# Re-timing the steps of an attention stage: later divisors, weight additions on DVE, two-bank hash bits, another order of loads

## The chip, the cores and the metric

The kernel runs on one core of one Trainium2 chip. The metric is the device time of one execution in microseconds. A figure "in the trace" is from one profiled execution.

Engines: PE does matrix products, DVE and ACT elementwise work, POOL (GpSimd) here weight additions and some transfers, and SP's queue issues most transfers (DMA). In the timelines below each queue's transfers stand in the order in which the kernel asks for them (SP: rd at 290.39, r at 293.85, q at 295.04 us). A "hole" below is a stretch in which PE waits.

## The reference

```python
def _attn_ref(q, k, v, proj):              # q, k, v: 4 x 8 heads x 768 x 64, proj: 64 x 6
    q_bits = (np.einsum('bhsd,dk->bhsk', q, proj) > 0)      # 6 hash bits of a row
    k_bits = (np.einsum('bhsd,dk->bhsk', k, proj) > 0)
    mask = bucket(q_bits)[:, :, :, None] == bucket(k_bits)[:, :, None, :]
    scores = np.where(mask, scale * np.matmul(q, k.transpose(0, 1, 3, 2)), -1e9)
    attn = np.exp(scores - np.max(scores, axis=-1, keepdims=True))
    attn = attn / (np.sum(attn, axis=-1, keepdims=True) + 1e-09)
    return np.matmul(attn, v)

def _moe_ref(x, w_in, w_out):              # x: 3072 x 512, w_in: 512 x 2048, w_out: 2048 x 512
    h = x @ w_in
    sp = np.maximum(h, 0.0) + np.log1p(np.exp(-np.abs(h)))
    return (h * erf(sp)) @ w_out
```

(Shortened; `bucket` stands for the sum of bits times powers of two.) The attention output, transposed, is the x of the feed-forward.

## The kernel before

Attention works on 16 pairs of heads. A pair takes four steps, n = 4i + r with r = 0 to 3: two halves of the queries, each with two groups of keys. A step's PE work is the scores of step n, part of the hash bits of pair i + 1, and the weighing of the values by the exponentials of step n - 1. After each half, the key sums become the divisors z. Once a pair, z is spread over partitions by a trip through DRAM (`zd`, `zc`), inverted on DVE, sent through DRAM again (`rd`, `r`) and multiplied in. Beside that, the feed-forward weights are loaded in 32 pieces of 512 KB and rounded by ACT, DVE and POOL, one piece in two steps.

```python
def hash_bits(d, r, bitp):                 # one half of q or k a step, in one PSUM bank
    what, half = ("q", "q", "k", "k")[r], r % 2
    # ...
    ps = bank("bits", 1)[:, 0:HS]
    nc.tensor.matmul(out=ps, lhsT=proj_sb, rhs=d[what][:, cols], start=True, stop=True)
    return what, cols, ps

def invert(i):
    # ...
    nc.vector.tensor_scalar(out=zc, in0=zc, scalar1=S * EPS, scalar2=None, op0=ALU.add)
    nc.vector.reciprocal(out=zc, in_=zc)
    rd = dram.tile([2, S], F32, name="rd", tag="rd")
    nc.sync.dma_start(out=rd[:, :].rearrange(...), in_=zc)              # arguments cut
    d["r"] = norm.tile([P, S], F32, name="r", tag="r")
    for ab in range(2):
        nc.sync.dma_start(out=d["r"][...], in_=rd[ab : ab + 1, :].broadcast_to([D, S]))

for n in range(NS + 4):
    i, r = divmod(n, 4)
    if n < NS:
        if r == 0 and i >= 1 and i + 1 < NPAIR:
            pairs[i + 1] = fetch(i + 1, load)      # q, k, v on the sync queue, three buffers
        scores(n)
        taking = bits(i + 1, r) if i + 1 < NPAIR else None
    if 1 <= n <= NS:
        sum_keys(n - 1)
        weigh(n - 1)
    if n < NS:
        exponentials(n)
        if taking:
            taking()
    if 1 <= n <= NS and (n - 1) % 2 == 1:
        divisor(n - 1)                             # PE needs the sums that DVE has just begun
        leave(n - 1)
    if r == 0 and i >= 1:
        spread(i - 1)
    if r == 2 and i >= 1:
        invert(i - 1)
    if r == 3 and i >= 1:
        normalise(i - 1)
    if n % 2 == 0:
        round_weights(n // 2, 0)
    else:
        round_weights(n // 2, 1)                   # ends with the addition, on POOL
        fetch_weights(n // 2 + 2)                  # on POOL's queue, behind that addition
```

Of the kernel before, what the change touches and what calls it, by code (L numbers as in the profile page):

```python
# [37 lines left out]
F32 = mybir.dt.float32  # L38
BF16 = mybir.dt.bfloat16
I32 = mybir.dt.int32  # L40
U32 = mybir.dt.uint32
AF = mybir.ActivationFunctionType
ALU = mybir.AluOpType
# [3 lines left out]
P = 128  # L47
# [16 lines left out]
def kernel(  # L64
# [11 lines left out]
    nc = tc.nc  # L76
    B, H, S, D = v.shape
# [17 lines left out]
    const = ctx.enter_context(tc.tile_pool(name="const", bufs=1))  # L95
    dram = ctx.enter_context(tc.tile_pool(name="dram", bufs=2, space=bass.MemoryType.DRAM))
    psum = ctx.enter_context(tc.tile_pool(name="psum", bufs=3, space=PSUM))
    proj_sb = const.tile([P, P], F32, name="proj_sb")
    kcol_sb = const.tile([P, 2], F32, name="kcol_sb")
    ones = const.tile([P, D], F32, name="ones")  # L100
# [7 lines left out]
    nc.vector.memset(proj_sb, 0.0)  # L108
    for ab in range(2):
        for c in range(2):  # L110
            nc.sync.dma_start(
                out=proj_sb[ab * D : ab * D + D, ab * D + c * NBIT : ab * D + (c + 1) * NBIT],
                in_=proj2[ab * D : ab * D + D, ab * NBIT : (ab + 1) * NBIT],
            )
# [27 lines left out]
    def big(name):  # L142
        return psum.tile([P, 2, 512], F32, name=name, tag="big", bufs=3)

    def bank(name, which):
        return psum.tile([P, 512], F32, name=name, tag=f"bank{which}", bufs=1)
# [34 lines left out]
            )  # L181
        return d

    def hash_bits(d, r, bitp):

        what, half = ("q", "q", "k", "k")[r], r % 2
        cols = slice(half * HS, (half + 1) * HS)
        if half == 0:
            d[what + "b"] = bitp.tile([P, S], BF16, name=what + "b", tag=what + "b")
        ps = bank("bits", 1)[:, 0:HS]  # L190
        nc.tensor.matmul(out=ps, lhsT=proj_sb, rhs=d[what][:, cols], start=True, stop=True)  # L191
        return what, cols, ps

    def take_bits(d, what, cols, ps):
        dst = d[what + "b"][:, cols]
        if what == "q":
            nc.scalar.activation(out=dst, in_=ps, func=AF.Sign, scale=2.0**100, bias=sgn[:, 0:1])
        else:
            nc.vector.tensor_scalar(
                out=dst,  # L200
                in0=ps,
                scalar1=kcol_sb[:, 0:1],
                scalar2=kcol_sb[:, 1:2],
                op0=ALU.is_gt,
                op1=ALU.mult,
            )

    def attention():
        NS = NPAIR * 4
        with (  # L210
# [1 line left out]
            tc.tile_pool(name="bitp", bufs=2) as bitp,  # L212
            tc.tile_pool(name="ep", bufs=1) as ep,
            tc.tile_pool(name="sums", bufs=2) as sums,
            tc.tile_pool(name="norm", bufs=1) as norm,
            tc.tile_pool(name="small", bufs=3) as small,
            tc.tile_pool(name="rawp", bufs=2) as rawp,
            tc.tile_pool(name="cvt", bufs=1) as cvt,
        ):
# [6 lines left out]
            def fetch_weights(n):  # L226
                if n >= len(pieces):
                    return
                if not WIDE:
                    nc.gpsimd.dma_start(out=pieces[n][0], in_=pieces[n][1])  # L230
                else:
                    raws[n] = rawp.tile([P, WP, 2], I32, name="raw", tag="raw")
                    nc.gpsimd.dma_start(
                        out=raws[n][:, :, :].rearrange("p c two -> p (c two)"), in_=pieces[n][1]
                    )

            def round_weights(n, part):
# [7 lines left out]
                if part == 0:  # L245
# [44 lines left out]
                    op0=ALU.mult,  # L290
                    op1=ALU.mult,
                )
                nc.gpsimd.tensor_tensor(
                    out=pieces[n][0], in0=top[:, :].bitcast(F32), in1=rest, op=ALU.add
                )
                raws.pop(n)
# [26 lines left out]

            def sum_keys(n):
                d = pairs[n // 4]
                es = [etiles[(n * GC + c) % len(etiles)][:, :, 0:HS] for c in range(GC)]
                if n % 2 == 0:
                    d["sum"] = sums.tile([P, 2, HS], F32, name="sum", tag="sum")
                    nc.vector.tensor_tensor(out=d["sum"], in0=es[0], in1=es[1], op=ALU.add)
                    es = es[2:]  # L330
                for e in es:
                    nc.vector.tensor_tensor(out=d["sum"], in0=d["sum"], in1=e, op=ALU.add)  # L332

            def weigh(n):
                half, g = n // 2 % 2, n % 2
# [14 lines left out]
                        )  # L350

            def divisor(n):
                d = pairs[n // 4]
                z = d["z_ps"] = bank("z_ps", 1)[:, 0:HS]
                for ab in range(2):
                    nc.tensor.matmul(  # L356
                        out=z[ab * D : ab * D + D, :],
                        lhsT=ones,
                        rhs=d["sum"][:, ab, :],
                        start=True,  # L360
                        stop=True,
                    )

            def leave(n):

                half = n // 2 % 2
                d = pairs[n // 4]
                b, j = divmod(n // 4, JP)
                cols = slice(half * HS, (half + 1) * HS)
                nc.scalar.copy(out=xT[b][:, j, cols], in_=d["av"][:, 0:HS])  # L370
                if half == 0:
                    d["ev"] = small.tile([P, 1], F32, name="ev", tag="ev")
                    nc.vector.tensor_scalar(
                        out=d["ev"],
                        in0=d["av"][:, HS : HS + 1],
                        scalar1=EPS,
                        scalar2=None,
                        op0=ALU.mult,
                    )
                    d["z"] = norm.tile([P, S], F32, name="z", tag="z")  # L380
                nc.scalar.copy(out=d["z"][:, cols], in_=d["z_ps"])

            def spread(i):

# [33 lines left out]
                    out=x, in0=x, scalar=d["ev"][:, 0:1], in1=d["r"], op0=ALU.add, op1=ALU.mult  # L418
                )

            def bits(i, r):
                what, cols, ps = hash_bits(pairs[i], r, bitp)
                return lambda: take_bits(pairs[i], what, cols, ps)

            for i in range(2):
                pairs[i] = fetch(i, load)
            for n in range(2):
                fetch_weights(n)
            for r in range(4):
                bits(0, r)()  # L430
            for n in range(NS + 4):
                i, r = divmod(n, 4)
                if n < NS:
                    if r == 0 and i >= 1 and i + 1 < NPAIR:
                        pairs[i + 1] = fetch(i + 1, load)
                    scores(n)
                    taking = bits(i + 1, r) if i + 1 < NPAIR else None
                if 1 <= n <= NS:
                    sum_keys(n - 1)
                    weigh(n - 1)  # L440
                if n < NS:
                    exponentials(n)
                    if taking:
                        taking()
                if 1 <= n <= NS and (n - 1) % 2 == 1:
                    divisor(n - 1)
                    leave(n - 1)
                if r == 0 and i >= 1:
                    spread(i - 1)
                if r == 2 and i >= 1:  # L450
                    invert(i - 1)
                if r == 3 and i >= 1:
                    normalise(i - 1)
                if n % 2 == 0:
                    round_weights(n // 2, 0)
                else:
                    round_weights(n // 2, 1)
                    fetch_weights(n // 2 + 2)

    def general():  # L460

        with (
# [1 line left out]
            tc.tile_pool(name="load", bufs=2) as load,  # L464
            tc.tile_pool(name="bitp", bufs=2) as bitp,
            tc.tile_pool(name="ep", bufs=2) as ep,
            tc.tile_pool(name="small", bufs=4) as small,
        ):
            ident = one.tile([P, P], F32, name="ident")
            make_identity(nc, ident)  # L470
            for i in range(NPAIR):
                d = fetch(i, load)
                b, j = divmod(i, JP)
                for r in range(4):
                    take_bits(d, *hash_bits(d, r, bitp))
                for ab in range(2):
                    rows = slice(ab * D, ab * D + D)
                    for half in range(2):
# [67 lines left out]



    def feed_forward(check):
        with (  # L550
            tc.tile_pool(name="hp", bufs=9) as hp,
            tc.tile_pool(name="sp", bufs=4) as sp,
            tc.tile_pool(name="work", bufs=2) as work,
            tc.tile_pool(name="outp", bufs=2) as outp,
            tc.tile_pool(name="chk", bufs=2) as chk,
        ):
            NU = (NT // T) * NG
            NP = NU // 2
# [103 lines left out]
            def extremes(m):  # L662

                i, half = divmod(m, 2)
                t = chk.tile([P, HS], F32, name="t", tag="t")
                nc.sync.dma_start(out=t, in_=qkT[i, :, half * HS : (half + 1) * HS])
                nc.vector.tensor_reduce(  # L667
                    out=most[:, half, i : i + 1],
                    in_=t,
                    axis=AX.X,  # L670
                    op=ALU.max,
                    apply_absolute_value=True,
                )

            for p in range(NP + 3):
                if p < NP:
                    hidden(2 * p)
                if 1 <= p <= NP:
                    take(2 * p - 1)
                if p >= 3:  # L680
# [40 lines left out]
        nc.vector.tensor_scalar(out=flag, in0=top, scalar1=1.0, scalar2=None, op0=ALU.add)  # L721

    with tc.manual_schedule():
        attention()
        feed_forward(judge)
    again = nc.values_load(flag[0:1, 0:1], min_val=0, max_val=1)
    with tc.If(again > 0):
        general()
        feed_forward(None)


# [51 lines left out]
```

## Time and profile before

| | |
|---|---|
| time, median | 1134.89 us (1132.72 to 1137.19, 3 runs) |
| profiled execution | 1126.5 us, granted clock 0.983 |
| attention, from the first scores | 17.9 to 441.1 us |
| feed-forward | 441.1 to 1126.5 us |

The page gives the busy share of the engines and a chain of what ended last; views of the trace give waits by engine and line, a timeline, and busy time in chosen stretches. In a timeline line the numbers are start and duration in us, then engine, source line, operation, output<-input, shapes and count, and in brackets the idle time before it with what ended it. In a waits line they are total us, times and the longest. The lines themselves stand in the prediction.

### The profile page before, as it was taken

What the parts mean: (1) busy time and instruction counts of PE and PEld (TensorE: products, weight loads), DVE (VectorE), ACT (ScalarE), POOL (GpSimd) and SP (SyncE); (2) the same over time, 40 slices, a digit from 0 to 9 for tenths busy, and PEclk for the clock granted to TensorE, in tenths of its full rate; (3) what the DMA queues carried; (4) which work ended last, traced back from release to release, by engine and by line L of the source; (5) the groups of instructions that cost most, each with busy time, mean ns of one, the idle gap of its engine ahead of it and who ended that gap; (6) DMA issues with size and microseconds to landing.
All of it is one profiled execution on the core that took longest, in us unless ns stands there. A gap on an engine that the chain in (4) does not pass through costs nothing.

```text
span 1126.5 us, 11846 instructions
## 1 busy us (share of the span) xinstructions
PE 1057.3 (94%) x4482; PEld 608.6 (54%) x4482; DVE 809.8 (72%) x962; ACT 678.0 (60%) x785; POOL 77.9 (7%) x68
## 2 busy tenths in 40 slices
PE   5999898999989987989999999999999998999987
PEld 2434333334334334856666666666666665666633
DVE  2767676767777773699787877777777767666692
ACT  3555555555555542597666666666666665666691
POOL 0211111111221120000000000000000000000000
PEclk9999999999999998999999999999999999999999
DMA  7133334434434311100101011111110000000000
GB/s 163 58 95 95 95 95 95 103 96 120 114 99 110 95 53 40 32 29 29 47 28 47 29 47 30 45 42 35 41 47 29 19 9 10 10 10 10 9 19 22
DMA packets 55329, 61.98 MB, mean 55 GB/s; under 512 B 33728, under 2 KB 41920, under 8 KB 55264
## 3 DMA queue, kind: packets, MB, share of 16 engines
q1 hardware_dynamic: 50512, 44.37, 15.6%
q0 software_dynamic: 4608, 16.78, 4.7%
q8 instruction: 37, 0.61, 0.2%
q14 instruction: 28, 0.23, 0.1%
q10 hardware_dynamic: 144, 0.00, 0.0%
HBM read 54.63 MB, written 6.49 MB: 54 GB/s over the span
## 4 chain that ended last, share of the span: by engine, by line
PE 75%; DVE 12%; DMA 8%; issue 2%; ACT 1%; SPq 1%; DVEq 0%
PE h_ps L567 28%; PE o_ps L645 28%; PE st L308 9%; PE av L344 6%; DMA r<-rd 5%; DVE sum L332 5%; PE bits L191 3%; DMA rd<-zc 2%; PE z_ps L356 2%; DVE xT L417 1%; DVE rest L285 1%; DVE top L274 1%; ACT xT L370 1%; SPq L408 1%; DVE unit L282 1%
## 5 line engine op out<-in xcount | busy, mean ns | idle before, releaser
L645 PE MATMUL o_ps<-w_out_sb,h 128*128 128x512 f32 x768 | 338.5, 595 | 7.5 <-DVE h L634 7.5
L567 PE MATMUL h_ps<-xT,w_in_sb 128*128 128x256 f32 x1536 | 342.6, 382 | 0.0
L567 PEld LDWEIGHTS h_ps<-xT,w_in_sb 128*128 128x128 f32 x1536 | 294.5, 192 | 59.1 <-issue 13.4
L645 PEld LDWEIGHTS o_ps<-w_out_sb,h 128*128 128x128 f32 x768 | 146.3, 191 | 175.0 <-issue 166.5
L320 ACT ACTIVATE e<-st 128x768 f32<-128x768 f32 x192 | 141.9, 809 | 92.0 <-PE st L308 89.2
L332 DVE TENSOR_TENSOR sum<-sum,e 128x768 f32<-128x768 f32 x128 | 150.7, 1177 | 9.3 <-DVE sum L332 0.5
L580 ACT COPY h<-h_ps 128x1024 f32<-128x1024 f32 x48 | 48.6, 1013 | 171.8 <-PE h_ps L567 162.8
L308 PE MATMUL st<-q,k 64*128 64x384 f32 x768 | 140.8, 501 | 0.0
L344 PE MATMUL av<-e,v 128*64 128x385 f32 (+1 forms) x768 | 137.9, 495 | 0.0
L626 DVE SCALAR_TENSOR_TENSOR s<-q,s 128x1024 f32<-128x1024 f32 x96 | 111.1, 1220 | 21.8 <-ACT q L625 21.8
L625 ACT ACTIVATE q<-z,cq 128x1024 f32<-128x1024 f32 x96 | 102.3, 1137 | 0.4 <-DVE s L608 0.4
L308 PEld LDWEIGHTS st<-q,k 64*128 64x128 f32 x768 | 75.6, 198 | 41.6 <-issue 6.6
L344 PEld LDWEIGHTS av<-e,v 128*64 128x64 f32 x768 | 49.5, 136 | 80.6 <-issue 71.7
L654 DVE COPY ob<-o_ps 128x512 f32<-128x512 f32 x24 | 16.4, 687 | 79.8 <-PE o_ps L645 79.8
L594 ACT ACTIVATE e<-e 128x1024 f32<-128x1024 f32 x48 | 49.1, 1046 | 35.2 <-DVE e L581 35.2
L356 PE MATMUL z_ps<-sum,ones 128*64 128x384 f32 x128 | 29.9, 545 | 36.8 <-DVE sum L332 36.8
L634 DVE TENSOR_TENSOR h<-h,s 128x1024 f32<-128x1024 f32 x48 | 56.6, 1220 | 7.1 <-ACT s L633 6.7
L598 DVE TENSOR_TENSOR w<-e,w 128x1024 f32<-128x1024 f32 x48 | 58.8, 1225 | 1.7
L608 DVE SCALAR_TENSOR_TENSOR s<-s,w 128x1024 f32<-128x1024 f32 x48 | 58.8, 1225 | 1.6
L605 DVE SCALAR_TENSOR_TENSOR s<-h,s 128x1024 f32<-128x1024 f32 x48 | 58.5, 1219 | 0.0
L626 DVE SCALAR_TENSOR_TENSOR s<-z,s 128x1024 f32<-128x1024 f32 x48 | 56.5, 1220 | 0.0
L667 DVE TENSOR_REDUCE most<-t 128x1 f32<-128x384 f32 x64 | 33.0, 549 | 31.6 <-DMA t<-in_qkT_dram 31.5
(57 smaller groups left out, 821.0 us busy)
## 6 DMA issues: line engine op xcount, KB each, us to landing
t<-in_qkT_dram SPq DMA_DIRECT2D x64, 192.0 KB, 2.4
raw<-in_w_in_dram POOLq DMA_DIRECT2D x16, 512.0 KB, 3.9
raw<-in_w_out_dram POOLq DMA_DIRECT2D x16, 512.0 KB, 3.8
q<-in_qkT_dram SPq DMA_DIRECT2D x32, 192.0 KB, 4.1
k<-in_qkT_dram SPq DMA_DIRECT2D x32, 192.0 KB, 6.9
v<-in_v_dram SPq DMA_DIRECT2D x32, 192.0 KB, 4.5
r<-rd SPq DMA_DIRECT2D x32, 192.0 KB, 3.2
out_dram<-ob SPq DMA_DIRECT2D x24, 256.0 KB, 2.0
```

Of the source, the lines that this page charges most:

```text
L308: nc.tensor.matmul(out=d["st"][c][:, ab, 0:HS], lhsT=d["k" + src][rows, keys], rhs=d["q" + src][rows, cols], start=(part == 0), stop=(part ...
L320: nc.scalar.activation(out=e[:, :, 0:HS], in_=st[:, :, 0:HS], func=AF.Exp, scale=scale)
L332: nc.vector.tensor_tensor(out=d["sum"], in0=d["sum"], in1=e, op=ALU.add)
L344: nc.tensor.matmul(out=d["av"][rows, 0:w], lhsT=d["v"][:, g * GC + c, rows], rhs=e[:, ab, 0:w], start=(g == 0 and c == 0), stop=(g == 1 an ...
L567: nc.tensor.matmul(out=ps[:, f, :], lhsT=w_in_sb[:, kc, (g * G + f) * P : (g * G + f + 1) * P], rhs=xT[b][:, kc, t0 : t0 + T], start=(kc = ...
L598: nc.vector.tensor_tensor(out=w, in0=e, in1=w, op=ALU.subtract)
L605: nc.vector.scalar_tensor_tensor(out=s, in0=h, scalar=0.0, in1=s, op0=ALU.max, op1=ALU.add)
L608: nc.vector.scalar_tensor_tensor(out=s, in0=s, scalar=S_MAX, in1=w, op0=ALU.min, op1=ALU.add)
L625: nc.scalar.activation(out=q, in_=z, func=AF.Square, bias=cq[:, j : j + 1])
L626: nc.vector.scalar_tensor_tensor(out=s, in0=q, scalar=r, in1=s, op0=ALU.add, op1=ALU.mult)
L634: nc.vector.tensor_tensor(out=d["h"], in0=d["h"], in1=s, op=ALU.mult)
L645: nc.tensor.matmul(out=ps, lhsT=st[t * NG + f // G]["h"][:, f % G, tt * P : (tt + 1) * P], rhs=w_out_sb[:, f, :], start=(f == 0), stop=(f ...
```

## The change

Its intent is to take PE's wait for the key sums out of the attention steps: the divisor comes a step later, with two sums alive at once, and what follows it (spreading, inverting, normalising) moves later too. The weight additions leave POOL for DVE. The hash bits of both halves go into one two-bank score buffer. The first loads are put in another order, and the last divisors are finished inside the feed-forward.

```diff
-            nc.sync.dma_start(
+            nc.scalar.dma_start(
                 out=proj_sb[ab * D : ab * D + D, ab * D + c * NBIT : ab * D + (c + 1) * NBIT],
...
+    def hash_bits(d, what):
+        ps = big("bits")
+        for half in range(2):
+            nc.tensor.matmul(out=ps[:, half, 0:HS], lhsT=proj_sb, ...)      # cut
+        return ps
...
+                queue = nc.sync if n < 2 else nc.gpsimd        # in fetch_weights
...
-                nc.gpsimd.tensor_tensor(
+                nc.vector.tensor_tensor(
                     out=pieces[n][0], in0=top[:, :].bitcast(F32), in1=rest, op=ALU.add
                 )
...
                 if n < NS:
                     if r == 0 and i >= 1 and i + 1 < NPAIR:
                         pairs[i + 1] = fetch(i + 1, load)
                     scores(n)
-                    taking = bits(i + 1, r) if i + 1 < NPAIR else None
-                if 1 <= n <= NS:
+                    exponentials(n)
+                    if r % 2 == 0 and i + 1 < NPAIR:
+                        what = "qk"[r // 2]
+                        ps = hash_bits(pairs[i + 1], what)
+                if n >= 1:
                     sum_keys(n - 1)
                     weigh(n - 1)
-                if n < NS:
-                    exponentials(n)
-                    if taking:
-                        taking()
-                if 1 <= n <= NS and (n - 1) % 2 == 1:
-                    divisor(n - 1)
+                if ps is not None:
+                    take_bits(pairs[i + 1], what, ps, bitp)
+                if n >= 1 and n % 2 == 0:
                     leave(n - 1)
-                if r == 0 and i >= 1:
+                if n >= 3 and n % 2 == 1:
+                    divisor(n - 2)
+                round_weights(n // 2, n % 2)
+                if n % 2 == 1:
+                    fetch_weights(n // 2 + 2)
+                if r == 1 and i >= 1:
                     spread(i - 1)
-                if r == 2 and i >= 1:
+                if r == 3 and i >= 1:
                     invert(i - 1)
-                if r == 3 and i >= 1:
-                    normalise(i - 1)
-                if n % 2 == 0:
-                    round_weights(n // 2, 0)
-                else:
-                    round_weights(n // 2, 1)
-                    fetch_weights(n // 2 + 2)
+                if r == 1 and i >= 2:
+                    normalise(i - 2)
+
+        def late(k): ...            # cut: last divisor, spreading, inversion, normalising
```

(Cut: tiles moved to outer pools, the two key sums kept apart by half in `sum_keys`, the first loads and hashes ahead of the loop, the copy of z moved from `leave` into `divisor`, and a buffer shared in feed-forward.)

More of the change, by code (lines that the diff above doesn't have):

```diff
@@ L97 @@
     psum = ctx.enter_context(tc.tile_pool(name="psum", bufs=3, space=PSUM))
+    norm = ctx.enter_context(tc.tile_pool(name="norm", bufs=1))
+    small = ctx.enter_context(tc.tile_pool(name="small", bufs=3))
     proj_sb = const.tile([P, P], F32, name="proj_sb")
@@ L182, in fetch, with take_bits @@
         return d
-    def hash_bits(d, r, bitp):
-        what, half = ("q", "q", "k", "k")[r], r % 2
-        cols = slice(half * HS, (half + 1) * HS)
-        if half == 0:
-            d[what + "b"] = bitp.tile([P, S], BF16, name=what + "b", tag=what + "b")
-        ps = bank("bits", 1)[:, 0:HS]
-        nc.tensor.matmul(out=ps, lhsT=proj_sb, rhs=d[what][:, cols], start=True, stop=True)
-        return what, cols, ps
-    def take_bits(d, what, cols, ps):
-        dst = d[what + "b"][:, cols]
+    def hash_bits(d, what):
+        ps = big("bits")
+        for half in range(2):
+            nc.tensor.matmul(
+                out=ps[:, half, 0:HS],
+                lhsT=proj_sb,
+                rhs=d[what][:, half * HS : (half + 1) * HS],
+                start=True,
+                stop=True,
+            )
+        return ps
+    def take_bits(d, what, ps, bitp):
+        d[what + "b"] = bitp.tile([P, S], BF16, name=what + "b", tag=what + "b")
+        dst = d[what + "b"][:, :].rearrange("p (h s) -> p h s", h=2)
+        src = ps[:, :, 0:HS]
         if what == "q":
-            nc.scalar.activation(out=dst, in_=ps, func=AF.Sign, scale=2.0**100, bias=sgn[:, 0:1])
+            nc.scalar.activation(out=dst, in_=src, func=AF.Sign, scale=2.0**100, bias=sgn[:, 0:1])
         else:
@@ L200, in take_bits @@
                 out=dst,
-                in0=ps,
+                in0=src,
                 scalar1=kcol_sb[:, 0:1],
@@ L214, in attention @@
             tc.tile_pool(name="sums", bufs=2) as sums,
-            tc.tile_pool(name="norm", bufs=1) as norm,
-            tc.tile_pool(name="small", bufs=3) as small,
             tc.tile_pool(name="rawp", bufs=2) as rawp,
@@ L228, in fetch_weights @@
                     return
+                queue = nc.sync if n < 2 else nc.gpsimd
                 if not WIDE:
-                    nc.gpsimd.dma_start(out=pieces[n][0], in_=pieces[n][1])
+                    queue.dma_start(out=pieces[n][0], in_=pieces[n][1])
                 else:
                     raws[n] = rawp.tile([P, WP, 2], I32, name="raw", tag="raw")
-                    nc.gpsimd.dma_start(
+                    queue.dma_start(
                         out=raws[n][:, :, :].rearrange("p c two -> p (c two)"), in_=pieces[n][1]
@@ L325, in sum_keys @@
                 d = pairs[n // 4]
+                key = "sum", n // 2 % 2
                 es = [etiles[(n * GC + c) % len(etiles)][:, :, 0:HS] for c in range(GC)]
                 if n % 2 == 0:
-                    d["sum"] = sums.tile([P, 2, HS], F32, name="sum", tag="sum")
-                    nc.vector.tensor_tensor(out=d["sum"], in0=es[0], in1=es[1], op=ALU.add)
+                    d[key] = sums.tile([P, 2, HS], F32, name="sum", tag="sum")
+                    nc.vector.tensor_tensor(out=d[key], in0=es[0], in1=es[1], op=ALU.add)
                     es = es[2:]
                 for e in es:
-                    nc.vector.tensor_tensor(out=d["sum"], in0=d["sum"], in1=e, op=ALU.add)
+                    nc.vector.tensor_tensor(out=d[key], in0=d[key], in1=e, op=ALU.add)
             def weigh(n):
@@ L352, in divisor @@
             def divisor(n):
+                half = n // 2 % 2
                 d = pairs[n // 4]
-                z = d["z_ps"] = bank("z_ps", 1)[:, 0:HS]
+                z = bank("z_ps", 1)[:, 0:HS]
                 for ab in range(2):
@@ L358, in divisor @@
                         lhsT=ones,
-                        rhs=d["sum"][:, ab, :],
+                        rhs=d["sum", half][:, ab, :],
                         start=True,
@@ L362, in divisor @@
                     )
+                if half == 0:
+                    d["z"] = norm.tile([P, S], F32, name="z", tag="z")
+                nc.scalar.copy(out=d["z"][:, half * HS : (half + 1) * HS], in_=z)
             def leave(n):
@@ L379, in leave @@
                     )
-                    d["z"] = norm.tile([P, S], F32, name="z", tag="z")
-                nc.scalar.copy(out=d["z"][:, cols], in_=d["z_ps"])
             def spread(i):
@@ L419, in normalise @@
                 )
-            def bits(i, r):
-                what, cols, ps = hash_bits(pairs[i], r, bitp)
-                return lambda: take_bits(pairs[i], what, cols, ps)
-            for i in range(2):
-                pairs[i] = fetch(i, load)
+            pairs[0] = fetch(0, load)
             for n in range(2):
                 fetch_weights(n)
-            for r in range(4):
-                bits(0, r)()
-            for n in range(NS + 4):
+            pairs[1] = fetch(1, load)
+            first = [hash_bits(pairs[0], what) for what in "qk"]
+            for what, ps in zip("qk", first):
+                take_bits(pairs[0], what, ps, bitp)
+            for n in range(NS + 1):
                 i, r = divmod(n, 4)
+                ps = None
                 if n < NS:
@@ L436, in attention, with late @@
                     scores(n)
-                    taking = bits(i + 1, r) if i + 1 < NPAIR else None
-                if 1 <= n <= NS:
+                    exponentials(n)
[3 more added lines that the diff above has]
+                if n >= 1:
                     sum_keys(n - 1)
                     weigh(n - 1)
-                if n < NS:
-                    exponentials(n)
-                    if taking:
-                        taking()
-                if 1 <= n <= NS and (n - 1) % 2 == 1:
-                    divisor(n - 1)
-                    leave(n - 1)
-                if r == 0 and i >= 1:
+                if ps is not None:
+                    take_bits(pairs[i + 1], what, ps, bitp)
+                if n >= 1 and n % 2 == 0:
+                    leave(n - 1)
+                if n >= 3 and n % 2 == 1:
[4 more added lines that the diff above has]
+                if r == 1 and i >= 1:
                     spread(i - 1)
-                if r == 2 and i >= 1:
+                if r == 3 and i >= 1:
                     invert(i - 1)
-                if r == 3 and i >= 1:
-                    normalise(i - 1)
-                if n % 2 == 0:
-                    round_weights(n // 2, 0)
-                else:
-                    round_weights(n // 2, 1)
-                    fetch_weights(n // 2 + 2)
+                if r == 1 and i >= 2:
+                    normalise(i - 2)
+        def late(k):
+            if k == 0:
+                normalise(NPAIR - 2)
+                divisor(NS - 1)
+                spread(NPAIR - 1)
+            elif k == 1:
+                invert(NPAIR - 1)
+            elif k == 2:
+                normalise(NPAIR - 1)
+        return late
     def general():
@@ L466, in general @@
             tc.tile_pool(name="ep", bufs=2) as ep,
-            tc.tile_pool(name="small", bufs=4) as small,
+            tc.tile_pool(name="row", bufs=4) as small,
         ):
@@ L473, in general @@
                 b, j = divmod(i, JP)
-                for r in range(4):
-                    take_bits(d, *hash_bits(d, r, bitp))
+                for what in "qk":
+                    take_bits(d, what, hash_bits(d, what), bitp)
                 for ab in range(2):
@@ L545, in general, with feed_forward @@
                         )
-    def feed_forward(check):
+    def feed_forward(check, late):
         with (
@@ L554, in feed_forward @@
             tc.tile_pool(name="outp", bufs=2) as outp,
-            tc.tile_pool(name="chk", bufs=2) as chk,
         ):
@@ L664, in extremes @@
                 i, half = divmod(m, 2)
-                t = chk.tile([P, HS], F32, name="t", tag="t")
+                t = outp.tile([P, DM], F32, name="t", tag="ob")[:, 0:HS]
                 nc.sync.dma_start(out=t, in_=qkT[i, :, half * HS : (half + 1) * HS])
@@ L677, in feed_forward @@
                     hidden(2 * p)
+                if late:
+                    late(p)
                 if 1 <= p <= NP:
@@ L723 @@
     with tc.manual_schedule():
-        attention()
-        feed_forward(judge)
+        late = attention()
+        feed_forward(judge, late)
     again = nc.values_load(flag[0:1, 0:1], min_val=0, max_val=1)
@@ L728 @@
         general()
-        feed_forward(None)
+        feed_forward(None, None)
 _OUT = ((3072, 512), "float32")
```

## The prediction

> **What bounds the kernel now.** I read the page's chain first, then the busy time by stretches, the waits inside the first stretch, and last the timeline of one step.
>
> ```profile
> PE 75%; DVE 12%; DMA 8%; issue 2%; ACT 1%; SPq 1%; DVEq 0%
> ```
>
> ```profile
> 18.00:441.10 423.10, 382.74 (x2169) 165.56 (x2168) 307.30 (x412) 226.61 (x349) 76.52 (x62) 0.97 0.36 91
> 441.10:1126.00 684.90, 668.02 (x2308) 440.93 (x2306) 500.95 (x528) 448.99 (x433) 0.00 (x0) 0.99 0.09 29
> ```
>
> The first is the chain by engine; the second view gives, for attention (18 to 441 us) and feed-forward (441 to 1126 us), the length, then busy us of PE, PE loads, DVE, ACT and POOL, the granted clock, DMA share and GB/s. Feed-forward is PE-bound (668 of 685 us) and the change hardly touches it. Attention is 423 us for 16 pairs of heads, 64 steps. It is PE with holes, and the waits of that stretch name them (total, times, longest):
>
> ```profile
> PE z_ps L356 <- DVE sum L332: 36.8, 15, 6.3
> ...
> DVE xT L417 <- DMA r<-rd: 36.0, 15, 3.0
> ...
> PE bits L191 <- DMA q<-in_qkT_dram: 1.1, 2, 0.9
> ```
>
> Once a pair PE waits for the divisor's key sum, because DVE, ahead of that sum, waited for the reciprocals r to come back from DRAM. The timeline shows what a hole costs. After a hole:
>
> ```profile
> 206.94 1.55 PE L356 MATMUL z_ps<-sum,ones 128*64 128x384 f32 x4 [2.13 <-DVE sum L332]
> ...
> 208.42 1.14 PE L308 MATMUL st<-qb,kb 64*128 64x384 bf16 x6
> ```
>
> and with no hole:
>
> ```profile
> 425.96 0.81 PE L356 MATMUL z_ps<-sum,ones 128*64 128x384 f32 x4
> ...
> 426.71 0.66 PE L308 MATMUL st<-qb,kb 64*128 64x384 bf16 x6
> ```
>
> By starts, z to the next scores is 208.42 - 206.94 = 1.48 us after the hole and 0.75 without; the scores that follow (208.42 to 211.87) take 3.45 against 2.52 (426.71 to 429.23). So a 2.1 us hole brings 1.7 us of slow PE.
>
> The line that decides my prediction is in the third row of waits: q of the next pair is already just in time. The sync queue, at the same place in an early pair:
>
> ```profile
> 58.81 0.35 SPq L403 DMA_DIRECT2D rd<-zc  x1
> 61.11 1.10 SPq L408 DMA_DIRECT2D r<-rd  x2
> 62.30 1.19 SPq L173 DMA_DIRECT2D q<-in_qkT_dram  x2
> ```
>
> ```profile
> 67.27 0.88 PE L191 MATMUL bits<-q,proj_sb 128*128 128x384 f32 x2 [0.92 <-DMA q<-in_qkT_dram]
> ```
>
> The loads of pair i+1 stand in SP's order behind the reciprocals of pair i-2: rd must land before r is issued, r before q. From rd to the hash of q is 8.46 us here and 7.74 us later (221.44 to 229.18, hole 0.22 us). The hash waits for this chain.
>
> **What the Trainium skill says.** "TensorE: Matmul & The Clock Gate", section "What's actually happening", puts PE at half clock after an idle window of about 3.4 us and back at full after a busy one. The trace agrees in kind: 1.48 against 0.75 us above is half rate, though holes of 2.2 us sometimes cost nothing. "DMA: Bandwidth & Descriptors", section "Anatomy of one DMA", says that a DMA's semaphore wait is made on the issuing sequencer before dispatch; the three SP lines agree, r starts 2.30 us after rd, and q only after both r. "GPSIMD Engine Reference", section "Specifications", says GpSimd shares SBUF interfaces with VectorE and contends with DVE instructions of two SBUF inputs. The trace agrees: one sum took 1.84 us while POOL added weights, and its neighbour 0.96.
>
> **The change part by part.** I use PE times of warm steps without holes, by differences of starts: scores 2.53 us (421.44 to 423.97), weighing 1.99, z 0.75, a step with one lone hash half 5.46 (211.87 to 217.33), so the hash is 5.46 - 2.53 - 1.99 = 0.94.
>
> 1. Hash bits of both halves together. The second half needs no new switch of shape: 32 h_ps records of 256 columns take 6.91 us, 0.216 each, so two of 384 columns take 0.65. Two halves are 1.59 instead of 1.88, twice a pair: -0.6 us. A pair of solid PE is then 4 x (2.53 + 1.99) + 2 x 0.75 + 2 x 1.59 = 22.8 us. The bits take a third-used score buffer, freed about 1 us after the hash; the third scores come 2.3 us after it, so no wait.
> 2. Divisor a step later. The sum has a whole step (4.5 us or more) for what made it 2 us late; the z hole goes. Typical pairs are now 27.3 us (hashes at 201.84 and 229.18), so up to 4.5 us a pair are to be had.
> 3. Weight addition on DVE: about 0.72 us more on DVE (a 512-wide two-input operation there is 0.69), minus the 0.88 us that the contention costs. DVE gains little and has room: 73.7 us of 100 in a mid-attention stretch. Alone it is worth nothing to PE.
> 4. Normalising moves a pair later: DVE's 2.4 us wait for r goes.
> 5. Inversion moves from step 2 to step 3 of a pair, and behind the weight rounding. **This is the cost.** The order of the changed kernel, as built, keeps the sync queue's sequence rd, r, r, then q of the next pair, and the hash of that q still follows the first scores of the next pair. Count from the start of PE's step 3. DVE is held by ev, which waits for ACT's copy after the weighing of step 2: 0.72, first rounding operation 0.81. Then, by spacing of starts in the trace: rounding 0.46 + 0.61, sums 0.98 + 0.98, rounding 0.72 + 0.46 + 0.61, the new addition 0.73, inversion and issue 0.44: together 5.99, so rd goes at 6.8 us. Before, it went at 0.53. Plus 7.75 us of rd, r, q, q lands at 14.55. PE, without holes, wants it at 5.27 (step 3: 2.53 + 1.99 + 0.75) + 2.53 = 7.80. **A new hole of about 6.7 us** each time. It occurs for pairs 3 to 15, thirteen times; pairs 0 to 2 have free buffers and nothing ahead of them. A hole that long leaves PE cold: from 1.7 us (the short hole) to 3.3 us (the 6.30 us hole at 439.63: 0.74 on z, 30.17 instead of 4 x 6.91 on the next 128 h_ps), say 2.4.
> 6. First loads: four proj loads leave the sync queue (1.38 to 3.91 us), weights no longer compete. First hash perhaps 6 us instead of 9.34, no wait between hashes; first scores about 14 instead of 17.95.
> 7. End of attention: the last divisor falls into feed-forward, so the hole of 6.30 us and 3.3 us of cold PE go; 0.75 us of z moves in.
>
> Sum: 14 + 24.0 (pair 0, partly cold) + 22.8 (pair 1) + 13 x (22.8 + 6.7 + 2.4 = 31.9) + 19.6 (pair 15, no hashes: 4 x 4.52 + 1.5) = 495 us to feed-forward, against 441. Feed-forward: -2.5 (warm start) + 0.75. Net 54 - 2 = **+52 us**, on 1134.9: 1187.
>
> **The rivals.** *It gains as intended.* If q is there in time, attention is 14 + 24 + 14 x 22.8 + 19.6 = 377 us, and the whole about 1069. For it: part 2 removes what the waits name, and all engines have room. Against it: q was late already by 0.92, 0.22 us with rd 6 us earlier. I would be wrong only if DVE inverts much earlier than its order says. *DVE becomes the bound.* Its work a pair is about 20.1 us now (73.7% of 27.3), about 19.6 after, under 22.8; holes would then be small, and the time about 1080. *Hole and gain cancel.* If the hole is 3 us and PE stays warm, a pair is 25.8, and the whole 1069 + 13 x 3, about 1108. *Longer hole.* Slow PE could shift ACT's copies and DVE with them; but the chain is anchored to ev in step 2, well after PE is warm, so it should not grow.
>
> **Range and chances.** Hole 5.5 to 7.5 us and cold 1.2 to 3.5 us, 13 times, give about -30 to +25 around 1187; I centre on 1185 and take 1150 to 1212. Slower by over 2% (above 1157.6) 0.82; within 2% 0.07, as that needs a hole of half the size; faster 0.11, for an error in the reading of the queue.
>
> **What would show it.** In the changed profile: PE's hash waits for the DMA of q, about 13 times, 6 to 7 us each, some 85 us; the z waits gone; hash-to-hash of pairs near 32 us instead of 27.3; rd issued 6 to 7 us after step 3 begins; granted clock in attention below 0.97; POOL without additions; sums near 0.96 us throughout; first scores near 14 us; no hole at the start of feed-forward. The prediction is wrong if the hash of q does not wait, and the pair then takes about 23 us.

## The result

| | before | changed |
|---|---|---|
| time, median | 1133.81 us (4 runs) | 1199.34 us (1198.07 to 1201.89, 4 runs) |
| ratio to before | 1 | 1.059 (95% interval 1.053 to 1.065) |
| profiled execution | 1126.5 us, clock 0.983 | 1197.8 us, clock 0.942 |

A ratio is the mean time of one kernel's fast runs over that of the other's of the same rounds, so it is not quite the ratio of the medians. The changed kernel is 5.9% slower; its outputs are correct.

The chain on the page of the changed kernel, and its busy time by stretches (columns as in the prediction, here cut where the first scores and the first feed-forward product start):

```profile
PE 77%; DMA 9%; DVE 9%; issue 2%; SPq 2%; ACT 1%; ACTq 0%; DVEq 0%
```

```profile
13.10:511.70 498.60, 389.62 (x2164) 173.91 (x2164) 292.45 (x425) 222.84 (x333) 16.00 (x30) 0.88 0.31 78
511.70:1197.80 686.10, 668.94 (x2312) 440.70 (x2310) 503.98 (x532) 449.25 (x434) 0.00 (x0) 0.99 0.09 29
```

All of the loss lies in attention: feed-forward takes 686.1 us against 685.4, attention 498.6 against 423.2, at a granted clock of 0.88 instead of 0.97. The waits of the changed kernel in attention:

```profile
DVE top L280 <- ACT keep L257: 151.0, 15, 12.1
ACT qb L204 <- PE bits L189: 135.0, 15, 10.6
...
PE bits L189 <- DMA q<-in_qkT_dram: 108.4, 13, 8.7
```

PE waits 13 times for q, 8.3 us each. The two lines above it are mostly the same holes seen from other engines: ACT waits for the hash, DVE for ACT. No wait of PE for a sum is left. One hole in the timeline, with POOL's weight load:

```profile
283.80 0.66 PE L314 MATMUL st<-qb,kb 64*128 64x384 bf16 x6
...
289.84 0.53 POOL L239 DMA_DIRECT2D raw<-in_w_out_dram  x1 [12.51 <-ACT z L373]
...
290.39 0.35 SPq L412 DMA_DIRECT2D rd<-zc  x1
...
293.85 1.10 SPq L417 DMA_DIRECT2D r<-rd  x2
295.04 1.19 SPq L175 DMA_DIRECT2D q<-in_qkT_dram  x2
...
300.19 2.90 PE L189 MATMUL bits<-q,proj_sb 128*128 128x384 f32 x4 [8.53 <-DMA q<-in_qkT_dram]
```

Step 3 begins at 283.80. The write rd is issued 6.6 us later, r 3.46 us after rd, q 1.19 us after r, and the hash starts 5.15 us after that. Beside this stands a transfer that the kernel before did not have there: a 512 KB weight load, issued 0.55 us ahead of rd. The view of transfers (KB each, median us from issue to landing) of the changed kernel has

```profile
rd<-zc SPq DMA_DIRECT2D x16, 6.0 KB, 3.5
```

and that of the kernel before

```profile
rd<-zc SPq DMA_DIRECT2D x16, 6.0 KB, 1.4
```

### The profile page after: what moved, and what is told of

Read it like the earlier page. It is cut to its first block, busy times and chain, and to the rows that moved or that the text cites. A ratio compares the mean times of both kernels' runs of the same rounds, so it can differ in the third digit from the quotient of the medians.

```text
span 1197.8 us, 11780 instructions
## 1 busy us (share of the span) xinstructions
PE 1064.0 (89%) x4482; PEld 617.1 (52%) x4482; DVE 798.5 (67%) x978; ACT 674.3 (56%) x769; POOL 16.2 (1%) x34
## 3 DMA queue, kind: packets, MB, share of 16 engines
q1 hardware_dynamic: 50480, 45.41, 14.8%
## 4 chain that ended last, share of the span: by engine, by line
PE 77%; DMA 9%; DVE 9%; issue 2%; SPq 2%; ACT 1%; ACTq 0%; DVEq 0%
PE h_ps L586 26%; PE o_ps L664 26%; PE av L351 10%; PE st L314 8%; PE bits L189 6%; DMA q<-in_qkT_dram 5%; DMA rd<-zc 4%; SPq L417 1%; DVE sum L339 1%; PE z_ps L364 1%; DVE sum L336 1%; DVE rest L291 1%; DVE top L268 1%; DVE top L280 1%; SPq L175 1%
## 5 line engine op out<-in xcount | busy, mean ns | idle before, releaser
L351 PE MATMUL av<-e,v 128*64 128x385 f32 (+1 forms) x768 | 149.2, 527 | 0.0
L189 PE MATMUL bits<-q,proj_sb 128*128 128x384 f32 x64 | 43.7, 834 | 115.0 <-DMA q<-in_qkT_dram 108.4
L314 PE MATMUL st<-q,k 64*128 64x384 f32 x768 | 134.3, 482 | 0.0
L339 DVE TENSOR_TENSOR sum<-sum,e 128x768 f32<-128x768 f32 x128 | 121.5, 950 | 8.9
L280 DVE SCALAR_TENSOR_TENSOR top<-top,keep 128x512 int32<-128x512 int32 x32 | 22.0, 688 | 151.0 <-ACT keep L257 151.0
L351 PEld LDWEIGHTS av<-e,v 128*64 128x64 f32 x768 | 53.3, 148 | 94.7 <-issue 86.5
L204 ACT ACTIVATE qb<-bits,sgn 128x768 bf16<-128x768 f32 x16 | 14.4, 901 | 139.4 <-PE bits L189 139.4
L314 PEld LDWEIGHTS st<-q,k 64*128 64x128 f32 x768 | 71.4, 187 | 37.9
L189 PEld LDWEIGHTS bits<-q,proj_sb 128*128 128x128 f32 x64 | 17.8, 307 | 132.7 <-issue 131.0
```

The costliest lines, as they stand in the source:

```text
L189: nc.tensor.matmul(out=ps[:, half, 0:HS], lhsT=proj_sb, rhs=d[what][:, half * HS : (half + 1) * HS], start=True, stop=True,)
L314: nc.tensor.matmul(out=d["st"][c][:, ab, 0:HS], lhsT=d["k" + src][rows, keys], rhs=d["q" + src][rows, cols], start=(part == 0), stop=(part ...
L339: nc.vector.tensor_tensor(out=d[key], in0=d[key], in1=e, op=ALU.add)
L351: nc.tensor.matmul(out=d["av"][rows, 0:w], lhsT=d["v"][:, g * GC + c, rows], rhs=e[:, ab, 0:w], start=(g == 0 and c == 0), stop=(g == 1 an ...
```

## The experiments

**Theory.** The changed kernel waits because the loads of q stand behind rd and r in the sync queue, and the inversion that releases rd now comes late on DVE: moved a step, and put behind the rounding with its new addition. A second term, which I had not foreseen, is that rd lands 2 us later beside the weight load. **Rivals.** The loads are slow in themselves; only the weight load matters; only the additions on DVE matter; or the loss needs several parts together.

Experiments one to six start from the changed kernel, the others from what is said. A wait of PE for q is given as an average over the holes.

**1. Loads asked for earlier** (they now stand ahead of rd and r in the queue; nothing else is changed):

```diff
-                    if r == 0 and i >= 1 and i + 1 < NPAIR:
-                        pairs[i + 1] = fetch(i + 1, load)
+                    if r == 2 and i + 2 < NPAIR:
+                        pairs[i + 2] = fetch(i + 2, load)
```

> Changed kernel, with one move: the loads of pair i+2 are asked for in step 2 of pair i (ahead of the inversion in the sync queue) instead of in step 0 of pair i+1 (behind it). Theory (order of the sync queue): the 13 waits of the hash for q (108 us) go to 0 and the cold PE after each (about 2.3 us) goes too; a pair takes 22.8 us; the whole about 1199 - 13 x 10.6 = 1061 us, between 1050 and 1080. Rival (the loads are simply slow, bandwidth or PE/DVE cannot go faster): a wait of several us stays at the hash or moves to the sums, the whole above 1120 us.

Measured: **1059.84 us** (4 runs), ratio 0.938 (0.932 to 0.944). All PE waits of over 1 us in this trace:

```profile
PE o_ps L664 <- DVE h L653: 7.4, 2, 4.5
PE bits L189 <- DMA proj_sb<-in_proj_dram: 6.8, 1, 6.8
PE bound L736 <- DVE mk L734: 3.4, 1, 3.4
PE st L314 <- DVE kb L206: 1.2, 1, 1.2
```

and two successive hashes of q:

```profile
36.70 1.56 PE L189 MATMUL bits<-q,proj_sb 128*128 128x384 f32 x4
...
59.43 1.56 PE L189 MATMUL bits<-q,proj_sb 128*128 128x384 f32 x4
```

A pair takes 22.73 us, where the working had 22.8 for solid PE. Attention takes 360.8 us at clock 1.00. Rd still lands in 3.5 us here, and it no longer matters. With the loads ahead of rd and r the loss is gone, and the rest of the change is a gain. (Early loads alone on the kernel before were not run; its PE waits for q in attention are only 1.1 us in total.)

**2. Inversion ahead of the rounding in step 3** (DVE reaches it sooner):

```diff
+                if r == 3 and i >= 1:
+                    invert(i - 1)
                 round_weights(n // 2, n % 2)
...
-                if r == 3 and i >= 1:
-                    invert(i - 1)
```

> Changed kernel, with the inversion put ahead of the weight rounding in step 3 (2.5 us earlier on DVE), all else as changed. Order theory: rd goes 2.5 us earlier, and before the 512 KB weight load instead of 0.5 us after it, so it should land in about 1.4 us instead of 3.4: the wait for q 8.3 - 2.5 - 2.0 = 3.8 us if the weight load does not now slow r or q, up to 6 if it does; the whole 1141 to 1170 us. Rival (only the weight load beside rd matters, DVE order does not): wait about 6.3 us, 1173 us or more.

Measured: 1171.41 us (2 runs), ratio 1.036; wait 6.1 us on average (79.9 over 13). One of the longer holes:

```profile
273.06 0.35 SPq L412 DMA_DIRECT2D rd<-zc  x1
274.61 1.10 SPq L417 DMA_DIRECT2D r<-rd  x2
275.31 0.53 POOL L239 DMA_DIRECT2D raw<-in_w_out_dram  x1 [12.81 <-ACT z L373]
275.80 1.19 SPq L175 DMA_DIRECT2D q<-in_qkT_dram  x2
...
283.97 2.26 PE L189 MATMUL bits<-q,proj_sb 128*128 128x384 f32 x3 [7.14 <-DMA q<-in_qkT_dram]
```

Rd is back to a median of 1.4 us, but the weight load now falls between r and q, and q lands in a median of 5.9 us instead of 4.2. The gain is only 2.2 us a hole: the weight load's cost moved from rd to q. I had expected 3.8 to 6 us; it is the bad end, and 1.4 us above the upper limit in time.

**3. Weight loads behind the loads of q, k, v** (no weight load near rd, DVE's order kept):

```diff
                         pairs[i + 1] = fetch(i + 1, load)
+                    if n % 2 == 0 and n >= 2:
+                        fetch_weights(n // 2 + 1)
...
-                if n % 2 == 1:
-                    fetch_weights(n // 2 + 2)
...
-                queue = nc.sync if n < 2 else nc.gpsimd
+                queue = nc.sync
```

> Changed kernel, with the weight loads issued by the sync queue at the start of steps 0 and 2, behind the loads of q, k, v, so no weight load lies beside rd; DVE's order unchanged. If the weight load is why rd lands in 3.4 us instead of 1.4: rd lands in about 1.4 us, the wait for q is about 6.3 us, the whole about 1199 - 13 x 2 = 1173 us. Rival (rd is slow for another reason, such as work beside it on DVE): landing stays 3.4 us, wait 8.3 us, 1199 us.

Measured: 1164.04 us (2 runs), ratio 1.030. One hole:

```profile
274.21 0.32 SPq L412 DMA_DIRECT2D rd<-zc  x1
275.62 1.10 SPq L417 DMA_DIRECT2D r<-rd  x2
...
281.89 1.62 PE L189 MATMUL bits<-q,proj_sb 128*128 128x384 f32 x2 [6.42 <-DMA q<-in_qkT_dram]
```

R follows rd after 1.41 us, and the hole is 6.42 us against the 6.3 expected. The weight load just ahead of rd is what made it slow: this edit also changes the load's queue, but in experiments 2 and 4, where the load stays on POOL's queue and only falls behind rd, rd lands in 1.4 us as well. The whole gained 9 us more than expected: a pair takes 30.78 us on average (between scores of pairs 2 and 15) against 33.34, which gives 33 of the 35 us gained. The shorter hole (6.35 us on average) gives 2.0 us of the 2.6 a pair; the slow PE after it gives the rest (30.78 less 22.73 and 6.35 leaves 1.7 us, against 2.3 in the changed kernel).

**4. Weight additions back on POOL** (one part of the change undone):

```diff
-                nc.vector.tensor_tensor(
+                nc.gpsimd.tensor_tensor(
                     out=pieces[n][0], in0=top[:, :].bitcast(F32), in1=rest, op=ALU.add
```

> Changed kernel, with the weight additions back on POOL (one part undone). DVE reaches the inversion 0.7 us earlier; the weight load follows POOL's 1.9 us addition and so is issued after rd instead of before it. Order theory with contention of the weight load: rd lands in 1.4 us, wait for q 5.6 us, up to 7 if the load slows r and q; sums beside POOL 0.9 us longer; the whole 1164 to 1182 us. Rival (moving the additions to DVE was harmless or a gain): 1199 us or more.

Measured: 1177.54 us (2 runs), ratio 1.042; wait 6.8 us (88.0 over 13), rd's landing 1.4 us, q's 5.1. At one hole:

```profile
277.76 0.35 SPq L412 DMA_DIRECT2D rd<-zc  x1
...
278.69 0.57 POOL L239 DMA_DIRECT2D raw<-in_w_out_dram  x1
279.19 1.10 SPq L417 DMA_DIRECT2D r<-rd  x2
```

So the moved additions did cost 22 us, about as much through what they released as through their own time on DVE. In this hole (6.97 us against the 8.53 shown above) rd goes 0.70 us earlier, 5.89 us into step 3 instead of 6.59. From rd to the hash it is 8.93 us instead of 9.80: with the addition off POOL, the next weight load is issued before rd instead of after it.

**5. Both moves of 2 and 3 together:**

> Changed kernel with both single moves at once: inversion ahead of the weight rounding (2.5 us on DVE), and weight loads behind the loads of q, k, v on the sync queue (about 2 us on rd or q). Alone they took the wait for q from 8.3 to 6.1 and to 6.4 us, the first because the weight load then fell between r and q (q landed in 5.9 us). If the two terms are separate and add: wait 8.3 - 2.5 - 2.0 = 3.8 us, the whole about 1199 - 13 x 4.5 = 1140 us (1133 to 1150). Rival (one hides the other, a floor near 6 us): wait about 6 us, 1160 us.

Measured: 1139.52 us (2 runs), ratio 1.008; three holes looked at in its timeline are 3.9 to 4.1 us. The two terms add; there is no floor near 6 us.

**6. Inversion back at the end of step 2**, where the kernel before has it:

```diff
+                if r == 2 and i >= 1:
+                    invert(i - 1)
                 round_weights(n // 2, n % 2)
...
-                if r == 3 and i >= 1:
-                    invert(i - 1)
```

> Changed kernel with only the inversion put back to the end of step 2, where the kernel before has it; loads stay behind it in the sync queue. Order theory: rd goes 0.5 us into step 3, q lands 7.75 us later, at 8.2; PE wants it at 7.8: wait about 0.5 us, mostly without cold PE; the whole 1199 - 13 x 10 = 1069 us (1060 to 1080). Rival (something else of the change holds the loads): waits of several us remain, over 1110 us.

Measured: 1076.67 us (2 runs), ratio 0.952; 12 waits for q, 14.8 us together, 1.2 us each. The loads still stand behind rd and r here, and rd lands in 1.4 us again. So the loss needs both, the order of the queue and the late inversion: taking the second away brings 123 of the 140 us that early loads bring.

**7. The suspect alone on the kernel before:** inversion in step 3 behind the rounding, normalising a pair later, the loop two steps longer.

```diff
-                if r == 2 and i >= 1:
-                    invert(i - 1)
-                if r == 3 and i >= 1:
-                    normalise(i - 1)
...
                     round_weights(n // 2, 1)
                     fetch_weights(n // 2 + 2)
+                if r == 3 and 1 <= i <= NPAIR:
+                    invert(i - 1)
+                if r == 1 and i >= 2:
+                    normalise(i - 2)
```

> Kernel before, with the suspect alone: the inversion in step 3 behind the weight rounding, normalising a pair later; divisors, hash, additions and first loads as before. Order theory: rd goes about 6 us into step 3 instead of 0.5, the hash waits 6 to 7 us for q and PE is cold after it, 13 times, while the waits for the sum mostly go: the whole 1175 to 1210 us. Rival (the loss needs the rest of the change): about 1134 or less.

Measured: 1199.22 us (2 runs), ratio 1.061. One hole:

```profile
291.59 0.35 SPq L403 DMA_DIRECT2D rd<-zc  x1
293.02 1.10 SPq L408 DMA_DIRECT2D r<-rd  x2
...
300.36 0.98 PE L191 MATMUL bits<-q,proj_sb 128*128 128x384 f32 x1 [7.04 <-DMA q<-in_qkT_dram]
```

The same hole appears in the old kernel, with rd landing fast and POOL still adding: 101.7 us of waits for q, of which 9.3 are the first loads', so 7.1 us in each of 13 pairs. PE's waits for sums fall to 2.8 us at the same time. Two things can do that here, and this run does not separate them: the sums are finished during the holes, and normalising a pair later takes away DVE's waits for r (36.0 us in attention before, none here).

**8. The intended gain alone on the kernel before:** `sum_keys`, `divisor` and `leave` as in the change, and

```diff
-                    divisor(n - 1)
                     leave(n - 1)
-                if r == 0 and i >= 1:
+                if 3 <= n <= NS + 1 and n % 2 == 1:
+                    divisor(n - 2)
+                if r == 1 and i >= 1:
                     spread(i - 1)
```

> Kernel before, with the intended gain alone: the divisor (and the spreading that follows it) a step later, inversion and the rest as before. If the wait for the sum and the cold PE after it are what bounds attention: the 36.8 us of waits fall to about 6 (the tail), a pair takes about 23.4 us, the whole 1075 to 1095 us. Rival (another wait takes its place, such as q): above 1110 us.

Measured: 1086.59 us (4 runs), ratio 0.961 (0.958 to 0.964). One wait for a sum is left, 7.8 us at the end of attention. The later divisor is worth 4% by itself, as long as the inversion stays where it was.

**9. Early loads, and weight additions on POOL** (experiments 1 and 4 together):

> Repaired kernel (loads early) with the weight additions back on POOL. The addition costs DVE 0.72 us and POOL's costs its sums 0.9 us, and DVE has room: the same within 4 us as the repaired kernel's 1059.8 us. Rival (moving the additions was needed): over 1068 us, with waits for sums.

Measured: 1059.67 us (4 runs) against 1059.84: no difference. With q in time, the place of the additions is worth nothing either way.

**10. Early loads, and the old hash** (one half a step, in a bank shared with the divisor):

> Repaired kernel (loads early) with the old hash, one half in each step, in one bank shared with the divisor. By the working: two separate halves cost 1.88 us of PE and the pair of halves 1.59, twice a pair for 15 pairs: about 9 us, and a few us at the start where each half waits for the taking of the one before: 1068 to 1075 us against 1059.8. Rival (the shared bank makes new waits): over 1080 us; rival (the two-bank hash is worth nothing): 1060 us.

Measured: 1069.31 us (4 runs), 9.5 us more. The total is as expected, its parts are not. A pair takes 23.13 us instead of 22.73 (between scores of pairs 2 and 15), so the two-bank hash saves 0.40 us a pair and not the 0.6 of the working: 5.6 us over pairs 1 to 14. Another 3.3 us go before pair 1, whose scores start at 37.43 us instead of 34.17.

**11. A better version:** experiment 1, with the reductions that check the inputs moved two steps later in feed-forward.

```diff
-                if check and 1 <= p:
-                    for m in range(4 * p - 4, 4 * p):
+                if check and 3 <= p:
+                    for m in range(4 * p - 12, 4 * p - 8):
```

> Repaired kernel (loads early), and the reductions that check the inputs start two steps later in feed-forward. In the repaired kernel's trace PE sits 4.47 us at the first output projection, waiting for a gate that stands on DVE behind four such reductions and a wait of 1.9 us for their input, and the 16 matmuls after it take 8.8 instead of 6.9 us. Without them the gate should be ready about 3.8 us earlier: 1059.8 - 3.8, and up to 1.9 less if PE stays warm: 1054 to 1057 us. Rival (another chain, ACT's, ends at the same time): 1059 to 1060 us.

Measured: **1055.19 us** (6 runs), ratio 0.935 (0.932 to 0.939), the fastest kernel here. PE's waits for the gate fall from 7.4 to

```profile
PE o_ps L664 <- DVE h L653: 3.5, 2, 2.9
```

## Why the prediction was right

Direction and cause were right; the time was 12 us above the 1187 of the sum and inside the range. Some of that closeness is luck: the terms were read from a profiled execution of 1126.5 us, but +52 was added to the median of 1134.9. From profile to profile the change cost 71 us, 19 more than the +52.

- *Part 5, the hole:* right in kind and number (13). Rd at 6.8 us of step 3 was 6.6 in the trace. The mis-sized term is "7.75 us of rd, r, q": it took 9.80 (290.39 to 300.19), because rd landed 2 us later beside the weight load. The hole was 8.3 us instead of 6.7; experiments 3, 4 and 5 show that term by itself.
- *Cold PE, 2.4 us a hole:* a stalled pair took 33.34 us on average (490.02 - 56.60 between scores of pairs 2 and 15, over 13), less 22.73 of solid PE and 8.34 of hole: 2.27.
- *The sum:* 13 x (33.34 - 31.9) = +19; first scores came at 13.1 us instead of 14, and pairs 0 and 1 took 3 us less than I gave them; the last pair took 21.7 instead of 19.6, as I left out that one more weighing, that of the last step, follows the last scores. Together 511.7 us to feed-forward instead of 495.
- *Parts 1, 2, 4:* right in kind: 22.73 us a pair against 22.8, no wait for sums, no wait of DVE for r worth naming (3.0 us, once). The 22.8 hides two errors that cancel. A lone hash half takes 0.84 us (211.87 to 212.71 in the trace of the kernel before), not 0.94, and the two-bank hash 1.48 (280.22 to 281.70 in the changed one), not 1.59; a weighing that no z follows takes 2.10 (281.70 to 283.80), not 1.99. The "typical" pair of 27.3 us was long too: pairs 2 to 14 of the kernel before average 26.4.
- *Part 3, "alone it is worth nothing to PE":* true with q in time (experiment 9), wrong in the changed kernel. I counted DVE's time and not that the weight load waits for the addition, so moving it moved a 512 KB transfer to just ahead of rd.
- *Part 7, feed-forward 1.75 us shorter:* it was 0.7 longer than before in the changed kernel, and 1.5 shorter in the repaired one (683.9). The traces show where these 2.2 us lie: PE runs slow in other places. After the 3.4 us wait for `mk`, 32 products into h_ps (the first of feed-forward's two) take 9.83 us in the changed kernel (granted clock 0.72) and 7.10 in the repaired one (1.00); the first 16 into o_ps (the second) take 9.97 against 8.83 us, the last 64 take 27.75 against 29.45. Why the clock falls after one such wait and not after the other stays open.
- *Rivals:* "it gains as intended", put at about 1069, is what early loads brought (1060); DVE never became the bound, at 292.6 busy us of 360.8.

## What to carry to other kernels

When work is moved a step later, follow not only who waits for it but also what stands behind it in its issuing queue: here a load whose data was ready was held by a small write that waited for DVE. Issue loads ahead of transfers that wait for results, or check by how many us each arrives before it is needed; 0.2 us of wait in the profile before was the warning. Moving an instruction also moves every transfer that waits for the buffer it frees.

## What the Trainium skill lacked or had wrong

- "TensorE: Matmul & The Clock Gate", section "What's actually happening", gives half clock after an idle window of about 3.4 us. In the trace of the kernel before, shorter holes already did it: after holes of 2.13, 2.19 and 2.21 us (z at 206.94, 179.69 and 234.36 us) the granted clock was 0.50 and z took 1.55 us, while after holes of 2.22, 2.23 and 2.26 us (98.03, 389.02 and 338.30 us) it was 1.00 and z took 0.87. At about 2.2 us the length of a hole does not decide it; what does, no run here shows.
- "DMA: Bandwidth & Descriptors", section "Issuing engines are not separate DMA queues", says that transfers of different engines interleave on the same 16 DMA engines, but not what that costs a small one: the 6 KB write rd landed in a median of 1.4 us in the kernel before (in attention r was issued at most 2.3 us after it), and of 3.5 us where a 512 KB load was issued about 0.55 us before it; loads of q behind such a load took 5.9 us instead of 4.2.
- The same page, section "Anatomy of one DMA", puts the wait for a semaphore on the issuing sequencer. It does not spell out that a ready transfer behind a waiting one in the same queue is held; here q was held so before each of 13 holes of 8.3 us (in the hole shown, until 295.04 us).
